# A 64-row remainder product for each of two weights, placed in the two halves of the TensorE array

## The chip, the cores and the metric

The kernel runs on one core of a Trainium2 chip. A core has TensorE (matrix products, called PE in the profile, with its weight loads shown apart as PEld), VectorE (DVE), ScalarE (ACT), GpSimd (POOL) and SyncE (SP, which issues transfers here). The metric is the device time of one execution in microseconds (us); less is better.

## The reference

A gated linear attention (an mLSTM) runs over 768 steps for 4 batches and 8 heads of width 40. Its output, 3072 rows of 320 features, goes through a bilinear layer.

```python
# per step t, for each batch and head (m is a running maximum for stability)
C = f_stab * C + i_stab * outer(v_t, k_t)
n = f_stab * n + i_stab * k_t
y_t = sigmoid(o_gate_t) * (C @ q_t) / maximum(abs(n @ q_t), 1.0)
...
x = y.transpose(0, 2, 1, 3).reshape(3072, 320)
out = ((x @ w_a) * (x @ w_b)) @ w_out        # w_a, w_b: 320 x 1536; w_out: 1536 x 320
```

The weights come as 64-bit floats.

## The kernel before

**Attention.** The 768 steps are cut into 6 chunks of 128 steps, which with 4 batches makes 24 pieces. Each piece goes through small stages: the scores (`stage_b`, or `begin_b` for the first six pieces, whose products contract over 40 rows in the upper or the lower half of the array), the product with v (`stage_c`, or `begin_c`), the part from the carried state (`stage_i`, or `begin_i`), the update of the state (`stage_u`, whose products have 64 columns), the gating (`stage_f`), and `stage_d`, which transposes the 320 features of 128 rows to features by rows.

**The layer.** `moe_block(kb)` handles one block of two or three pieces, so 256 or 384 rows of x; there are 9 blocks, three of them with 256 rows. The 1536 columns of the weights are cut into 12 slices of 128, numbered `ff`. For each slice `up(ff)` makes two sums in PSUM (`pu`): `acc[0]` for `w_a` and `acc[1]` for `w_b`. ScalarE (for two slices VectorE) copies `acc[0]` to `g`, VectorE multiplies `acc[1]` by it, and splits the product into `gh` and `gl`. Two slices later `down` multiplies those with `w_out` into the output's sums (`pd`).

**Two words per number.** TensorE takes rounded 32-bit words (float32r in the code, f32 in the profile). So x is held as `xh`, its rounded part, and `xl`, the remainder; a weight as a high and a low part. For each full tile of 128 features three products are made: high with `xh`, high with `xl`, low with `xh`. The product of low with `xl` is left out.

**The last 64 features.** 320 features are two tiles of 128 and 64 more. `stage_f` writes those 64 twice, one copy behind the other, so that the third tile of `xh` and of `xl` has them in rows 0 to 63 and again in rows 64 to 127:

```python
nc.scalar.copy(y[:, DM:], y[:, 2 * P:DM])
```

The third weight tile (`rests`) has, for `w_a`, the high part in rows 0 to 63 and the low part in rows 64 to 127, and for `w_b` the other way round:

```python
for j in range(2):
    rows, other = (slice(64 * i, 64 * i + 64) for i in (j, 1 - j))
    nc.scalar.copy(w[rows, j], W[rows])
    nc.vector.tensor_tensor(w[other, j], pc[rows], W[rows], op=ALU.add)
```

One full-height product of this tile with `xh` thus gives high and low at once. A second one with `xl` gives high with `xl`, and low with `xl` besides. Each `up(ff)` has 2 x 8 = 16 products.

**Order.** `moe_block` and the attention are generators. The main loop takes one step of `moe_block` (one product) at a time and, by a running count (`acc += units / (total * 0.93)`, where `total` is 12 x (16 + 3 x pieces)), steps of the attention in between. The framework's scheduler then settles the order of each engine's instructions from what has been written and a model of time. PSUM for `pu` is a ring of three banks.

Of the kernel before, what the change touches and what calls it, by code (L numbers as in the profile page):

```python
# [20 lines left out]
def kernel(  # L21
# [82 lines left out]
    x = ident[0:BH, 0:BH].rearrange("k (x j) -> k x j", j=2)  # L104
# [245 lines left out]
    def w_up(ff, kt, j):  # L350

        cols = slice(ff % 3 * P, (ff % 3 + 1) * P)
        if kt == 2:
            return ws[STAGES * (ff // 3) + 4][:, j, cols]
        w = ws[STAGES * (ff // 3) + 2 * kt + j]
        return w[:, 0, cols], w[:, 1, cols]

    def w_down(ff):
        w = ws[STAGES * (ff // 3) + 5 + ff % 3]
        return w[:, 0], w[:, 1]  # L360
# [3 lines left out]
    def need(x):  # L364

        while ready[0] < x:
            next(conv)
# [398 lines left out]
    def moe_block(kb):  # L766
        NT = sizes[kb] * P
        xh, xl = (x[..., 0:NT] for x in xt.pop(kb))
        pd = [ps_dn.tile([P, 512], F32, tag=f"pd{t}", name=f"pd{kb}_{t}") for t in range(sizes[kb])]
        gs = {}  # L770

        def down(ff):
            need(STAGES * (ff // 3) + 6 + ff % 3)
            gh, gl = gs.pop(ff)
            for t in range(sizes[kb]):
                cols = slice(t * P, (t + 1) * P)
                wh, wl = w_down(ff)
                for a, w, first, last in (
                    (gh, wh, True, False), (gh, wl, False, False), (gl, wh, False, True)
                ):  # L780
                    nc.tensor.matmul(  # L781
                        pd[t][:, 0:DM], a[:, cols], w,
                        start=(ff == 0 and first), stop=(ff == NF - 1 and last),
                    )
                    yield
            if ff == NF - 1:
                for t in range(sizes[kb]):
                    c, b = chunks[begins[kb] + t]
                    o = mpool.tile([P, NTB], F32, tag="acp", name=f"o{kb}_{t}")[:, 0:DM]
                    nc.scalar.copy(o, pd[t][:, 0:DM])  # L790
                    nc.sync.dma_start(out[b * S + c * P:b * S + (c + 1) * P, :], o)

        def up(ff):
            need(STAGES * (ff // 3) + 5)
            busy = hot[0] > 0
            hot[0] -= 1
            acc = [
                ps_up.tile([P, NTB], F32, tag="pu", name=f"pu{kb}_{ff}_{j}")[:, 0:NT]
                for j in range(2)
            ]  # L800
            for j in range(2):
                terms = []
                for kt in range(2):
                    h, l = w_up(ff, kt, j)
                    terms += [(h, xh[:, kt, :]), (h, xl[:, kt, :]), (l, xh[:, kt, :])]

                h = w_up(ff, 2, j)
                terms += [(h, xh[:, 2, :]), (h, xl[:, 2, :])]
                for x, (a, r) in enumerate(terms):
                    nc.tensor.matmul(  # L810
                        acc[j], a, r, start=(x == 0), stop=(x == len(terms) - 1),
                    )
                    yield
                if j == 0:
                    g = mpool.tile([P, NTB], F32, tag="acp", name=f"g{kb}_{ff}")[:, 0:NT]
                    (nc.vector.tensor_copy if ff in [1, 2] else nc.scalar.copy)(g, acc[0])  # L816
            nc.vector.tensor_tensor(g, acc[1], g, op=ALU.mult)  # L817
            gh = mpool.tile([P, NTB], F32R, tag="gh", name=f"gh{kb}_{ff}")[:, 0:NT]
            nc.vector.tensor_copy(gh, g)  # L819
            gl = mpool.tile([P, NTB], F32R, tag="gl", name=f"gl{kb}_{ff}")[:, 0:NT]  # L820
            (nc.gpsimd if kb * 12 + ff < 16 else nc.vector).tensor_tensor(  # L821
                gl, g, gh.bitcast(F32), op=ALU.subtract
            )
            gs[ff] = (gh, gl)

        LAG = 2
        for ff in range(NF + LAG):
            if ff < NF:
                yield from up(ff)
            if ff >= LAG:  # L830
                yield from down(ff - LAG)
# [286 lines left out]
```

## Time and profile before

| | |
|---|---|
| median of three runs | 565.53 us (559.82 to 567.49) |
| the profiled execution's own time | 560.51 us |
| its span, first to last instruction | 558.5 us |
| TensorE clock granted, mean | 0.993 |
| PE busy | 544.9 us (98%), 4925 instructions |
| weight loads busy (PEld) | 518.0 us (93%) |
| VectorE busy | 389.4 us (70%) |
| ScalarE busy | 267.9 us (48%) |
| GpSimd busy | 126.9 us (23%) |

The profile shows one execution. Products overlap in the array, so a busy time of PE counts the overlap once, and a product's listed duration (0.33 us for 384 columns, say) is longer than the step from its start to the next one's start. It is the step that a stream of products costs. A plain float32 product (not the rounded kind) stands as two records. The difference between the execution's own time and the span, 2.0 us, lies around the first and the last instruction.

### The profile page before, as it was taken

The numbers are of one execution on the slowest core, as the hardware profiler recorded it, in microseconds if no ns is written. First come the engines' busy times: TensorE is split into PE (matmuls) and PEld (weight loads), VectorE is DVE, ScalarE is ACT, GpSimd is POOL, SyncE is SP. The second block draws the span as 40 slices with busy tenths as digits, with TensorE's granted clock in tenths as the row PEclk, the third lists the DMA queues.
The fourth block names the chain that finished last, engine by engine and source line by source line (L and its number), as shares of the span: only waits on it lengthen the run. The fifth ranks groups of instructions, "written<-read, shape, count | busy, mean of one in ns | idle before, by whom it ended". The sixth has DMA issues, their size and how long they took to land.

```text
span 558.5 us, 12726 instructions
## 1 busy us (share of the span) xinstructions
PE 544.9 (98%) x4925; PEld 518.0 (93%) x4925; DVE 389.4 (70%) x888; ACT 267.9 (48%) x645; POOL 126.9 (23%) x188
## 2 busy tenths in 40 slices
PE   8999999899999999999999999999999999999997
PEld 6898898799999899999989999998999999999997
DVE  6889999964858683968749774977757755944332
ACT  5574678752626761556525654644526733310111
POOL 3102414641232320332031330333021302000000
PEclk9799999999999999999999999999999999999999
DMA  9999941393649762569536684586539704200001
GB/s 191 215 263 291 290 72 51 94 179 71 108 103 193 141 139 58 123 142 180 107 99 156 108 151 115 118 145 138 118 97 154 144 0 115 48 1 25 0 1 35
DMA packets 198551, 66.75 MB, mean 120 GB/s; under 512 B 184220, under 2 KB 191772, under 8 KB 198492
## 3 DMA queue, kind: packets, MB, share of 16 engines
q1 hardware_dynamic: 198444, 65.86, 56.4%
q8 instruction: 38, 0.62, 0.5%
q14 instruction: 21, 0.17, 0.1%
q10 hardware_dynamic: 48, 0.10, 0.0%
HBM read 41.11 MB, written 5.95 MB: 84 GB/s over the span
## 4 chain that ended last, share of the span: by engine, by line
PE 60%; DMA 17%; DVE 10%; ACT 5%; issue 3%; SPq 3%; POOL 1%; ACTq 0%; DVEq 0%; POOLq 0%
PE pu L810 31%; PE pd L781 15%; DMA T<-qks 4%; DMA c_dram<-cb 3%; ACT gbc L490 3%; DMA va<-in_v_dram 2%; PE pV L603 2%; PE pU L628 2%; DVE gbc L554 2%; DMA gbc<-g_dram 1%; DMA raw<-in_moe_w_a_dram 1%; DVE pb L556 1%; PE pS L884 1%; PE pV L927 1%; PE pS L545 1%
## 5 line engine op out<-in xcount | busy, mean ns | idle before, releaser
L810 PE MATMUL pu<-xh,w 128*128 128x384 f32 (+1 forms) x1080 | 276.5, 324 | 2.6 <-ACT g L816 0.9
L810 PE MATMUL pu<-xl,w 128*128 128x384 f32 (+1 forms) x648 | 208.0, 322 | 0.0
L810 PEld LDWEIGHTS pu<-xh,w 128*128 128x128 f32 x1080 | 190.6, 189 | 5.9 <-ACT g L816 1.3
L781 PE MATMUL pd<-w,gh 128*128 128x320 f32 x576 | 126.7, 309 | 0.0
L810 PEld LDWEIGHTS pu<-xl,w 128*128 128x128 f32 x648 | 122.2, 189 | 0.2
L817 DVE TENSOR_TENSOR g<-pu,g 128x384 f32<-128x384 f32 (+1 forms) x108 | 54.6, 505 | 89.4 <-PE pu L810 46.3
L781 PEld LDWEIGHTS pd<-w,gh 128*128 128x128 f32 x576 | 96.7, 188 | 0.1
L781 PE MATMUL pd<-w,gl 128*128 128x320 f32 x288 | 85.3, 310 | 0.0
L816 ACT COPY g<-pu 128x384 f32<-128x384 f32 (+1 forms) x90 | 39.6, 440 | 93.4 <-PE pu L810 84.2
L490 ACT ACTIVATE gbc<-gbc,gtab 128x128 f32<-128x128 f32 x160 | 49.1, 389 | 18.1 <-POOL gbc L483 18.0
L821 DVE TENSOR_TENSOR gl<-g,gh 128x384 fp32r<-128x384 f32 (+1 forms) x92 | 52.2, 568 | 1.9
L781 PEld LDWEIGHTS pd<-w,gl 128*128 128x128 f32 x288 | 53.1, 188 | 0.2
L585 POOL TENSOR_TENSOR vw<-va,gtab 128x336 f32<-128x336 f32 x20 | 16.4, 822 | 160.3 <-PE pU L628 135.2
L819 DVE CAST gh<-g 128x384 fp32r<-128x384 f32 (+1 forms) x108 | 41.1, 382 | 2.2
L483 POOL TENSOR_SCALAR_AFFINE_SELECT gbc<-gbc 128x1024 f32<-128x1024 f32 x20 | 22.6, 1132 | 65.1 <-DMA gbc<-g_dram 32.9
L554 DVE TENSOR_TENSOR gbc<-gbc,pb 128x512 f32<-128x512 f32 x36 | 27.2, 757 | 6.8 <-ACT pb L552 6.6
L603 PEld LDWEIGHTS <-pb 128*128 128x128 bf16 x576 | 23.4, 96 | 6.4 <-DVE pb L556 3.2
L684 POOL TENSOR_TENSOR osig<-osig,den 128x320 f32<-128x320 f32 x22 | 16.6, 754 | 54.9 <-DVE den L671 42.9
L603 PE MATMUL pV<-va,pb 128*128 128x42 bf16 x288 | 25.9, 183 | 2.7 <-DVE pb L556 2.7
L790 ACT COPY o<-pd 128x320 f32<-128x320 f32 x24 | 8.8, 434 | 40.3 <-PE pd L781 40.3
L550 DVE TENSOR_TENSOR gbc<-pS,gbc 128x512 f32<-128x512 f32 x36 | 23.7, 682 | 4.0 <-PE pS L545 4.0
L518 ACT COPY qks<-qks 128x640 bf16<-128x640 bf16 x36 | 26.0, 725 | 0.6
(154 smaller groups left out, 849.6 us busy)
## 6 DMA issues: line engine op xcount, KB each, us to landing
gbc<-g_dram SPq DMA_DIRECT2D x20, 512.0 KB
q<-in_q_dram SPq DMA_DIRECT2D x24, 160.0 KB
k<-in_k_dram SPq DMA_DIRECT2D x24, 160.0 KB
va<-in_v_dram SPq DMA_DIRECT2D x24, 160.0 KB
osig<-in_o_gate_dram SPq DMA_DIRECT2D x24, 160.0 KB
raw<-in_moe_w_out_dram SPq DMA_DIRECT2D x12, 320.0 KB
out_dram<-o SPq DMA_DIRECT2D x24, 160.0 KB
raw<-in_moe_w_a_dram SPq DMA_DIRECT2D x8, 384.0 KB
```

The lines of the kernel that those rows point to most:

```text
L483: nc.gpsimd.affine_select(E, E, pattern=[[0, H], [1, P]], compare_op=ALU.is_ge, fill=-1e30, base=0, channel_multiplier=-1,)
L490: nc.scalar.activation(E[:, h], E[:, h], AF.Exp, bias=beta[:, h:h + 1])
L518: nc.scalar.copy(qks[:, 0, :, lo:lo + 2 * D], qks[:, 1, :, D - lo:3 * D - lo])
L550: nc.vector.tensor_tensor(E, pS, E, op=ALU.mult)
L554: nc.vector.tensor_tensor(E, E, pb[:, 0], op=ALU.subtract)
L603: nc.tensor.matmul(pv[:, h], pb[i][:, h % HH, :], vb[j][:, h], start=(x == 0), stop=(x == len(terms) - 1),)
L781: nc.tensor.matmul(pd[t][:, 0:DM], a[:, cols], w, start=(ff == 0 and first), stop=(ff == NF - 1 and last),)
L810: nc.tensor.matmul(acc[j], a, r, start=(x == 0), stop=(x == len(terms) - 1),)
L816: (nc.vector.tensor_copy if ff in [1, 2] else nc.scalar.copy)(g, acc[0])
L817: nc.vector.tensor_tensor(g, acc[1], g, op=ALU.mult)
L819: nc.vector.tensor_copy(gh, g)
L821: (nc.gpsimd if kb * 12 + ff < 16 else nc.vector).tensor_tensor(gl, g, gh.bitcast(F32), op=ALU.subtract)
```

## The change

For the third tile, the product of the weights with `xl` no longer uses all 128 rows. For `w_a` it takes rows 0 to 63 of the weights and of `xl`, for `w_b` rows 64 to 127: the high part alone in each case. The program gives these products half-height tiles of 64 x 128 at array row 0 and at row 64. The one for `w_a` stays the last of its sum; the one for `w_b` is now the first of its own sum, and no step of the generator lies between the two, so they are written one behind the other. The number of products stays 16 for each slice; the generator's steps for a slice fall from 16 to 15 (`total` is not changed).

```diff
                 h = w_up(ff, 2, j)
-                terms += [(h, xh[:, 2, :]), (h, xl[:, 2, :])]
+                rows = slice(64 * j, 64 * j + 64)
+                half_k = [(h[rows], xl[rows, 2, :])]
+                terms = terms + [(h, xh[:, 2, :])]
+                terms = terms + half_k if j == 0 else half_k + terms
                 for x, (a, r) in enumerate(terms):
                     nc.tensor.matmul(
                         acc[j], a, r, start=(x == 0), stop=(x == len(terms) - 1),
                     )
-                    yield
+                    if j == 1 or x < len(terms) - 1:
+                        yield
```

**TensorE in the last block, slice 5** (names are sum slice and weight, `pu_5_0` for `w_a` and `pu_5_1` for `w_b`, then the moving operand and the weight tile). Before:

```order
L810 MATMUL pu_5_0_7782<-xl_7092,w_849 128x384
L810 MATMUL pu_5_0_7782<-xh_7091,w_849 128x384
L810 MATMUL pu_5_0_7782<-xh_7091,w_869 128x384
L810 MATMUL pu_5_0_7782<-xl_7092,w_869 128x384
L810 MATMUL pu_5_1_7783<-xh_7091,w_839 128x384
L810 MATMUL pu_5_1_7783<-xl_7092,w_839 128x384
L810 MATMUL pu_5_1_7783<-xh_7091,w_839 128x384
```

Here the fourth row is the full-height product of the third tile with `xl` for `w_a`; that for `w_b` ends its own sum, four rows further on. In the changed program the same place reads:

```order
L813 MATMUL pu_5_0_7782<-xl_7097,w_845 128x384
L813 MATMUL pu_5_0_7782<-xh_7096,w_845 128x384
L813 MATMUL pu_5_0_7782<-xh_7096,w_865 128x384
L813 MATMUL pu_5_0_7782<-xl_7097,w_865 128x384
L813 MATMUL pu_5_1_7783<-xl_7097,w_865 128x384
L813 MATMUL pu_5_1_7783<-xh_7096,w_835 128x384
L813 MATMUL pu_5_1_7783<-xl_7097,w_835 128x384
```

The fourth and the fifth row are now the two half-height products, side by side, with full-height products ahead and behind. In 68 of the 108 slices they stand like this: 51 with 384 columns and 17 with 256.

**TensorE in a middle block, slice 4** (`pd` is the output's sum, `pb` and `pV` are the attention's). Before:

```order
L810 MATMUL pu_4_0_3703<-xh_2541,w_869 128x384
L810 MATMUL pu_4_0_3703<-xl_2542,w_869 128x384
L810 MATMUL pu_4_1_3704<-xh_2541,w_839 128x384
L810 MATMUL pu_4_1_3704<-xl_2542,w_839 128x384
L810 MATMUL pu_4_1_3704<-xh_2541,w_839 128x384
```

After the change:

```order
L813 MATMUL pu_4_0_3689<-xh_2544,w_865 128x384
L813 MATMUL pu_4_0_3689<-xl_2545,w_865 128x384
L781 MATMUL pd_0_3257<-w_815,gh_2_3508 128x320
L813 MATMUL pu_4_1_3690<-xl_2545,w_865 128x384
L813 MATMUL pu_4_1_3690<-xh_2544,w_835 128x384
L813 MATMUL pu_4_1_3690<-xl_2545,w_835 128x384
```

The scheduler has moved another block product, full height, between the two half-height ones. In 40 of the 108 slices something of that kind stands between them (one product in 14 slices, up to 98 rows of attention in one): 21 with 384 columns and 19 with 256.

## The prediction

> **What bounds the kernel.** I read the page first, then the chain that ended last, then what PE waited for, then rows of PE in order of time.
>
> ```profile
> span 558.5 us, 12726 instructions
> ...
> PE 544.9 (98%) x4925; PEld 518.0 (93%) x4925; DVE 389.4 (70%) x888; ACT 267.9 (48%) x645; POOL 126.9 (23%) x188
> ```
>
> PE is busy for 98% of the span and no other engine for more than 70%. Since products overlap, that alone does not say that PE streams at its best pace, so the chain of the last block is needed (start, length, what):
>
> ```profile
> 543.73 2.80 PE pu L810 x16
> 546.53 1.31 PE pd L781 x9
> 547.84 2.80 PE pu L810 x16
> ```
>
> One slice of a 384-column block is 16 + 9 products and takes 547.84 - 543.73 = 4.11 us, with nothing else on the chain. One of the 16 costs 2.80 / 16 = 0.175 us. Time put into or taken out of PE there moves the end one for one. How much slack is left elsewhere is in the list of waits (total us, times, longest):
>
> ```profile
> PE pV L603 <- DVE pb L556: 2.7, 5, 0.9
> ...
> PE pX L707 <- DVE gbc L550: 1.0, 2, 0.7
> PE pu L810 <- ACT g L816: 0.9, 1, 0.9
> PE pu L810 <- DVE g L817: 0.7, 2, 0.4
> ```
>
> These four are 5.3 us in 10 waits, all that PE waits for in the layer and the main attention but for parts of a microsecond. So the kernel is bound by PE nearly throughout, and the question is what the half-height products cost on PE.
>
> **Two half-height products side by side.** The early attention already runs them: L884 contracts over 40 rows, in the upper or lower half (start, length, what):
>
> ```profile
> 7.53 0.38 PE L884 MATMUL pS<-T 40*128 40x128 f32 x2 [0.39 <-ACT T L873]
> ...
> 7.53 1.16 PE L884 MATMUL pS<-T 40*128 40x128 f32 x16 [0.39 <-ACT T L873]
> ...
> 60.47 1.16 PE L884 MATMUL pS<-T,T 40*128 40x128 f32 x8
> ...
> 480.62 0.28 PE L810 MATMUL pu<-xh,w 128*128 128x256 f32 x1
> 480.74 1.07 PE L545 MATMUL pS<-T,T 120*128 120x128 bf16 x16
> ```
>
> At 7.53 products alternate between the halves, and 16 records take 1.16 us. At 60.47 all are in one half, and 8 records take the same 1.16 us. The first two records at 7.53 fit in 0.38 us although one lasts 0.373 (the longest duration in the next fence), so the second starts some 0.007 us after the first. At full height the 16 records of 128 columns at 480.74 start (1.07 - 0.22) / 15 = 0.057 us apart, 0.22 being the length of one. So a pair in the two halves does overlap, and its second product is nearly free: I take 0.006 us. The bound on the other side, since no rounded 32-bit product runs like this before, is one after the other, 0.174 us at 384 columns and 0.12 at 256.
>
> The Trainium skill, TensorE: Matmul & The Clock Gate, section The mechanism of its part on packing, has tiles in different rows start about 4 ns apart, which this row bears out; by it the second product would cost 0.004 us.
>
> **Going to half height and back.** Now the price of entering and leaving. First 256 columns, then 384; in the second place the other tile has 64 columns instead of 64 rows, the nearest row that follows a 384-column product:
>
> ```profile
> 86.15 0.28 PE L810 MATMUL pu<-xl,w 128*128 128x256 f32 x1
> 86.27 0.40 PE L810 MATMUL pu<-xh,w 128*128 128x256 f32 x2
> 86.51 0.28 PE L810 MATMUL pu<-xl,w 128*128 128x256 f32 x1
> 86.72 0.49 PE L884 MATMUL pS<-T,T 40*128 40x128 f32 x2
> 87.13 0.41 PE L781 MATMUL pd<-w,gh 128*128 128x320 f32 x1
> ...
> 158.90 0.34 PE L810 MATMUL pu<-xh,w 128*128 128x384 f32 x1
> 159.07 0.34 PE L810 MATMUL pu<-xl,w 128*128 128x384 f32 x1
> 159.34 0.92 PE L628 MATMUL pU<-vw,k 128*64 128x42 f32 x16
> 160.19 0.62 PE L810 MATMUL pu<-xh,w 128*128 128x384 f32 x2
> ...
> 158.90 0.19 PEld L810 LDWEIGHTS pu<-xl,w 128*128 128x128 f32 x1
> 159.34 0.80 PEld L628 LDWEIGHTS pU<-vw,k 128*64 128x64 f32 x16 [0.25 <-issue]
> 160.19 0.30 PEld L810 LDWEIGHTS pu<-xh,w 128*128 128x128 f32 x2
> ...
> L884 PE MATMUL pS<-T,T x64: 272/272/373, 32.8 to 89.2; 40*128 40x128 f32 x64
> ```
>
> (The last row is that line's shortest, median and longest duration in ns.) A visit to the other tile shape has four prices:
>
> - Entry, emptying the array. Full-height products of 256 columns start 0.12 us apart (86.15 to 86.51 is three steps); the half-height one starts 0.21 after the last: **+0.09**. With 384 columns 0.17 becomes 0.27: **+0.10**. In both the next start is the product's own length less 0.07.
> - Entry, the load. In the stream the weights of the next product are loaded under the running one: the PEld row at 158.90 is for the product at 159.07. The load at 159.34 begins only with its product. The first L884 after an entry lasts 373 ns instead of 272: **+0.10**.
> - Leaving, emptying. The two records at 86.72 cost 0.11 each (60.47: (1.16 - 0.27 - 0.10) / 7) and the first one's load 0.10; the next product starts after 0.41: **+0.09**. By the rule of the entry a 384-column product would pay +0.10.
> - Leaving, the load. At 160.19 the two products last 0.62 together; less 0.34 the second starts after 0.28 instead of 0.17: **+0.11**.
>
> Together 0.39 to 0.41 us a visit. I take 0.385 at 256 and 0.40 at 384 columns. The type of the numbers is not the cause: at 480.62 a 32-bit product is followed by a bf16 one after 0.12 us, the plain step.
>
> The Trainium skill, TensorEngine Tiling (Array Packing), section Key Properties, says the same against this change: "Changing tiling mode (not just tile) drains the TensorE". The rows above agree. The page prices neither the drain nor the load behind it; with a drain alone (0.18 to 0.20 us) the sum would be that of the second rival.
>
> **The sum.** The order of the changed program has the two half-height products adjacent in 68 slices and apart in 40.
>
> - Visits: 68 for the adjacent pairs, 2 x 40 for the others, less 3 that lie against a half-height product of the attention: 145. Of them 93 have 384 columns (51 + 42), 52 have 256 (17 + 38 - 3). 93 x 0.40 + 52 x 0.385 = **+57.2 us**.
> - Saved: only adjacent pairs overlap. 51 x (0.174 - 0.006) + 17 x (0.12 - 0.006) = **-10.5 us**. Apart, a half-height product streams as many columns as a full one and saves nothing.
> - The product of the low weights with `xl` that disappears had no instruction of its own: nothing.
> - The generator makes 12 x 24 = 288 steps in a 384-column block instead of 300, so the attention is dealt out 4% later. PE's own work beside it hides that: the attention's waits in the list are 3.7 us. Uncovered, it would be a few more of those, 0.5 to 0.9 us each.
> - Waits: no new one in steady state. `w_b`'s sum needs its bank one product earlier; in a ring of three it was freed by a copy a whole slice (4.11 us) before. ScalarE's copy and VectorE's product come later with PE and have idle time. Of the 5.3 us of waits above some go, since PE comes later to what it waited for: between 0 and -5.3, I take **-3 us**.
>
> 57.2 - 10.5 - 3 = +43.7. From the profiled execution's 560.5 us that is 604.2. The median of the three runs was 5.0 above that execution and the lowest 0.7 below; I add half of the five, less rounding: **606 us**, 7% slower than 565.5.
>
> **Rivals.**
>
> - *Not side by side after all*: the rounded products run one after the other although in two halves; then the change does not do what it says. The saved 10.5 us are gone: about 617. Against it stand the starts at 7.53; for it, that two 128-column streams in sequence (2 x 0.057) would also fit the 0.11 us at which pairs go on there.
> - *The load hides*: the half-height weights and those behind them are loaded while the array empties. Each visit costs 0.18 to 0.20 instead of 0.39: 93 x 0.20 + 52 x 0.18 = 28 less 10.5, so +17.5, and with the same 2.5 for the median 579 (-1 for waits). The PEld rows at 159.34 and 160.19 speak against it.
> - *The other side, no emptying*: between two rounded 32-bit products with the same weight tile the array goes over to half height in the running stream, as it does from bf16 to 32 bits. Then only the saving is left: 560.5 - 10.5 = 550, with 2.5 for the median 552.5, 2.3% faster. It decides below 10.5 / 145 = 0.07 us a visit. Every entry and exit quoted speaks against it, but none has rounded products on both sides.
> - *The waits take more*: all 5.3 us and part of the start go. About 602; inside the forecast.
>
> The Trainium skill, same page, section Theoretical Speedup, gives "Up to 2×" for a contraction of at most 64 rows; taken alone that is the third rival. The trace agrees only while the shape stays, as at 7.53.
>
> **How the numbers follow.** Forecast 0.74, with 597 to 614 from visits of 0.37 to 0.42 us and waits of 0 to -5.3. Not side by side 0.09, load hidden 0.09, no emptying 0.04, and 0.04 for new waits beyond 622. The range 588 to 622 takes in the first two and leaves out 0.17. Two per cent, 11 us, is about what a measurement of this kernel tells from no change. Faster by more than that: the third rival, 0.03 of its 0.04. Within: its rest and part of the second, 0.05. Slower 0.92.
>
> **What would show it.** Rows of L813 with 64*128, two of them 0.35 us long together with 384 columns and more by the load's 0.1; a start 0.27 us behind the product ahead; a first full product of about 0.44 us after each. In the last block 4.11 us per slice should become 4.11 + 0.40 - 0.17 = 4.34 where the two are adjacent, 4.11 + 0.80 = 4.91 where not. PE's busy share stays near 98%, since emptying counts as busy; PEld's falls. The prediction is wrong if half-height loads start under the product ahead, if a pair's two starts lie 0.17 apart, or if the attention falls behind and PE's waits grow beyond some 10 us.

## The result and the profile after

| | before | after |
|---|---|---|
| median of four runs | 563.87 us | 598.25 us (594.87 to 605.76) |
| the profiled execution | 560.51 us | 600.5 us |
| span | 558.5 us | 598.7 us |

The change makes the kernel **slower: ratio 1.059, 95% interval 1.047 to 1.071**. The forecast was 606 us, 588 to 622. One of the four executions after, at 605.76, was a slow one that the ratio leaves out.

The first lines of the page, and what became of the half-height products in the view of groups that keeps shapes apart:

```profile
span 598.7 us, 12729 instructions
...
PE 587.5 (98%) x4925; PEld 513.8 (86%) x4925; DVE 392.5 (66%) x888; ACT 269.2 (45%) x645; POOL 126.3 (21%) x188
...
PEclk9999979999999999999999999999999999999999
...
L813 PE MATMUL pu<-xl,w 64*128 64x384 f32 x144 | 41.0, 439 | 0.0
```

PE has as many instructions as before and is again busy for 98% of a span that is 40 us longer. Its weight loads are busy for less (86% against 93%): time has gone in which nothing is loaded. A half-height product of 384 columns lasts 0.439 us on average, a full one in the stream 0.34. PEclk is the granted clock of TensorE in tenths of full speed, in forty slices of the span.

The chain of the last block, where PE has nothing else to do (start, length, what):

```profile
583.52 3.03 PE pu L813 x15
586.55 1.31 PE pd L781 x9
587.86 3.03 PE pu L813 x15
```

A slice now takes 587.86 - 583.52 = 4.34 us, and it took 4.11. The 16 products of `up` stand here as 15, since two start together, but need 3.03 us where 16 needed 2.80. Where the 0.23 us lie is seen in the rows of PE and of the weight loads, in order of time, in the same block:

```profile
584.25 0.51 PE L813 MATMUL pu<-xh,w 128*128 128x384 f32 x2
584.70 0.44 PE L813 MATMUL pu<-xl,w 64*128 64x384 f32 x2
585.07 0.44 PE L813 MATMUL pu<-xh,w 128*128 128x384 f32 x1
585.35 0.34 PE L813 MATMUL pu<-xl,w 128*128 128x384 f32 x1
...
584.08 0.37 PEld L813 LDWEIGHTS pu<-xh,w 128*128 128x128 f32 x2
584.69 0.19 PEld L813 LDWEIGHTS pu<-xl,w 64*128 64x128 f32 x2 [0.25 <-issue]
585.07 0.19 PEld L813 LDWEIGHTS pu<-xh,w 128*128 128x128 f32 x1 [0.18 <-issue]
585.17 0.19 PEld L813 LDWEIGHTS pu<-xl,w 128*128 128x128 f32 x1
```

Two half-height products of 0.44 us fit into 0.44 us: their starts are less than 0.01 us apart, and so are their two loads. That part works. But the product ahead started at 584.25 + 0.51 - 0.34 = 584.42 or so, and the pair 0.27 behind it; the next full product starts 0.37 behind the pair, and the one after it 0.28 later. A plain step is 0.174. The idle times of the weight loads, 0.25 and 0.18 us with no release named, are the two stretches in which I take the array to empty: no weights come in and no product starts. The first product on either side then lasts 0.44 instead of 0.34; its load starts with it and not under the product ahead.

What PE waited for (total us, times, longest):

```profile
PE pd L781 <- POOL gl L825: 2.3, 1, 2.3
...
PE pu L813 <- ACT g L820: 0.8, 1, 0.8
...
PE pX L707 <- ACT cst L633: 0.3, 1, 0.3
```

Of the four waits that the list before had with 5.3 us in all, those for `pb` and `gbc` are gone, and those for `g` are down to one of 0.8 us. The 2.3 us on GpSimd's `gl` are new and lie in the first block, at 68 us. Behind this wait the granted clock is at half for 10.24 us, from 72.3 on: there products of 256 columns start 0.21 us apart, not 0.12. Before, the clock is at half for 6.8 us too, but at 18.6 us, ahead of the layer's first product.

### The profile page after: what moved, and what is told of

Same layout as the page of the kernel before. It is cut to its first block, busy times and chain, and to the rows that moved or that the text cites. A ratio compares the mean times of both kernels' runs of the same rounds, so it can differ in the third digit from the quotient of the medians.

```text
span 598.7 us, 12729 instructions
## 1 busy us (share of the span) xinstructions
PE 587.5 (98%) x4925; PEld 513.8 (86%) x4925; DVE 392.5 (66%) x888; ACT 269.2 (45%) x645; POOL 126.3 (21%) x188
## 4 chain that ended last, share of the span: by engine, by line
PE 91%; issue 3%; DVE 3%; ACT 1%; POOL 1%; DMA 1%; ACTq 0%; POOLq 0%; DVEq 0%
PE pu L813 51%; PE pd L781 22%; PE pV L603 4%; PE pS L545 3%; PE pU L628 2%; PE pX L707 1%; PE pS L888 1%; PE pI L571 1%; PE pV L931 1%; PE pc L449 1%; PE pI L908 1%; PE pT L874 1%; DMA g_i<-in_i_gate_dram 1%; PE pc L450 1%; DVE cr L426 0%
## 5 line engine op out<-in xcount | busy, mean ns | idle before, releaser
L813 PE MATMUL pu<-xh,w 128*128 128x384 f32 (+1 forms) x1080 | 285.5, 334 | 0.0
L813 PE MATMUL pu<-xl,w 128*128 128x384 f32 (+3 forms) x648 | 202.0, 355 | 0.8 <-ACT g L820 0.8
L813 PEld LDWEIGHTS pu<-xl,w 128*128 128x128 f32 (+1 forms) x648 | 109.8, 188 | 29.0 <-issue 20.7
L781 PE MATMUL pd<-w,gh 128*128 128x320 f32 x576 | 132.0, 317 | 0.5 <-DVE gh L823 0.5
L823 DVE CAST gh<-g 128x384 fp32r<-128x384 f32 (+1 forms) x108 | 39.0, 361 | 2.0
L483 POOL TENSOR_SCALAR_AFFINE_SELECT gbc<-gbc 128x1024 f32<-128x1024 f32 x20 | 24.1, 1203 | 49.4 <-DMA gbc<-g_dram 48.1
L603 PEld LDWEIGHTS <-pb 128*128 128x128 bf16 x576 | 23.5, 96 | 4.3 <-issue 3.1
L686 ACT COPY osig<-osig 128x64 f32<-128x64 f32 x22 | 5.4, 244 | 48.3 <-DVE osig L685 48.1
```

Of the source, the lines that this page charges most:

```text
L483: nc.gpsimd.affine_select(E, E, pattern=[[0, H], [1, P]], compare_op=ALU.is_ge, fill=-1e30, base=0, channel_multiplier=-1,)
L603: nc.tensor.matmul(pv[:, h], pb[i][:, h % HH, :], vb[j][:, h], start=(x == 0), stop=(x == len(terms) - 1),)
L781: nc.tensor.matmul(pd[t][:, 0:DM], a[:, cols], w, start=(ff == 0 and first), stop=(ff == NF - 1 and last),)
L813: nc.tensor.matmul(acc[j], a, r, start=(x == 0), stop=(x == len(terms) - 1),)
```

## The experiments

Three theories were set against each other. **A**: every visit to the half height costs about 0.39 us, and a pair side by side gives 0.17 back. **B**: the moved order (40 slices with work between the two, another dealing of the attention) made the loss. **C** says that the two halves do not overlap.

**The change with full-height products again.** One line of the changed kernel:

```diff
-                half_k = [(h[rows], xl[rows, 2, :])]
+                half_k = [(h, xl[:, 2, :])]
```

> The changed kernel with both remainder products at full height again: they stay the last product of w_a's sum and the first of w_b's, and the generator makes the 15 steps a slice of the change. TensorE's order agrees with that of the change in 99 of 100 products, and no product of the layer is half-height. Theory A (0.39 us for each visit): the time of before, 558 to 566 us, so that the whole loss of the change lies in the visits. Theory B (the moved order has a part in it, as it had when both products were put at the slice's end): between 570 and 598.

Measured: 563.3 us against 561.2 for the kernel before, ratio 1.004 (1.000 to 1.008). So the order and the 15 steps account for some 2 us of the 34, for 5 at most by the interval, and theory B falls as the cause of the loss. Between this kernel and the change only the height of two products in 16 differs, and in one product of 100 the order that the scheduler chose. What the order does cost lies in the first block: in the profiled execution the second block begins 4.7 us later than before (114.86 against 110.13 us), and from there to the end the two differ by 0.2 us. The wait for `gl` is here too, and behind it the clock at half, from 68.8 us on, again for 10.24 us:

```profile
PE pd L781 <- POOL gl L825: 2.7, 1, 2.7
...
PEclk9999969999999999999999999999999999999999
```

**Half height in the order of before.** Here the program's order of products is that of before throughout, and each remainder product stays last in its own sum, so no pair forms.

```diff
-                terms += [(h, xh[:, 2, :]), (h, xl[:, 2, :])]
+                rows = slice(64 * j, 64 * j + 64)
+                terms += [(h, xh[:, 2, :]), (h[rows], xl[rows, 2, :])]
```

> The order of before, each remainder product last in its own sum, but half-height: 216 visits less a few, no pair. Theory A: 72 x 2 x 0.40 + 36 x 2 x 0.385 = 85 paid, less up to 8 of waits: 637 to 650 us. Theory B: the time of before, 560 to 570. Were the price the emptying alone (0.18 to 0.20): 600 to 607.

Measured: 632.2 us, ratio 1.130 (1.124 to 1.137), 72 us slower. Then the same with `w_a`'s product alone (`rows` is all 128 for `j == 1`):

> The order of before to the instruction, and only w_a's remainder product half-height: 108 visits, no pair. Theory A: half of what 216 visits cost in this order, 72 x 0.40 + 36 x 0.385 = 42.7 less up to 6 of waits: 596 to 604 us. If the first visit of a slice did the damage and the second came cheap (a rival to a price per visit): 610 or more. If waits hid the first visits: below 590.

Measured: 592.9 us, ratio 1.057 (1.051 to 1.062), 32 us slower: 108 visits cost 32, 216 cost 72. Both miss the expected range by 3 to 5 us on the cheap side. The chains of the last block, first with two visits to a slice, then with one:

```profile
614.08 3.38 PE pu L811 x16
617.45 1.51 PE pd L781 x9
618.96 3.38 PE pu L811 x16
```

```profile
570.82 3.20 PE pu L811 x16
574.02 1.31 PE pd L781 x9
575.34 3.20 PE pu L811 x16
```

4.88 us and 4.52 us a slice, beside 4.11 with none: 0.77 for two visits and 0.41 for one in these rows, 0.39 a visit over the whole block. So where PE alone sets the time the price per visit is as forecast, and the shortfall lies elsewhere. Measured from the first product of each block to that of the next, the last block grows by 9.4 us with 24 visits and by 4.75 with 12, which is 0.39 to 0.40 each; blocks 2 to 5 (numbered from 0) grow by 7.4 to 8.0 and by 2.8 to 3.5. There 1.2 to 2.1 us in a block are hidden, whether 12 or 24 visits are paid. Those are blocks with attention, and before, PE waited in them.

**Both at the slice's end, full height.** The next three kernels put the two remainder products last in the slice and issue them together, so that nothing can come between:

```diff
+            with tc.issue_after(last), tc.high_priority(4000):
+                for j in range(2):
+                    product(j, 7, *ends[j])
```

> Both remainder products stand at the end of the slice, side by side, as full-height products: no visit to the half height, 83 stretches of equal tile shape in the program's order against 81 before. Theory A (the price is 0.39 us for each visit to the half height, the gain 0.168 us for each overlapped pair of 384 columns and 0.114 of 256): no change from before, 560 to 567 us. Theory B (the loss comes from the moved order and the changed dealing of the attention): still clearly slower than before, above 575.

Measured: 583.5 us, ratio 1.039 (1.031 to 1.047). A miss for theory A, and the number lies where B had it. But this is not the change's order, which at full height cost little; it is an order with a loss of its own. `acc[0]` ends 7 products later, so its copy to `g` comes late, and PE waits for it:

```profile
PE pu L802 <- ACT g L822: 7.3, 7, 1.9
PE pc L449 <- ACT g L822: 2.4, 1, 2.4
...
PEclk9799989799999999999999998999999899999999
```

The granted clock, 0.978 over the span against 0.993 before, dips in five of the forty slices of the span, where it dipped in one before: it is at half there for 3.4 or 6.8 us at a time. So the next two are to be compared with this kernel and with each other, and the last block tells more than the whole.

**All 108 pairs together.**

> The same order as with full-height products at the slice's end, but in the two halves; all 108 pairs stand together: 108 visits. Theory A: 72 x 0.40 + 36 x 0.385 = 42.7 paid, 72 x 0.168 + 36 x 0.114 = 16.2 saved, so 26 above the full-height version less up to 6 of waits that go: 583 to 592 us, faster than the change by 8 to 14. Theory B: as the full-height version in this order. Theory C (the two halves do not overlap): 600 to 606.

Measured: 598.7 us, ratio 1.069 (1.064 to 1.074). Outside the expected 583 to 592, for the base itself stands 20 us higher than I took it. Above that base it is 15 us, where 20 to 26 were expected; where the rest went was not traced. The last block:

```profile
580.79 3.03 PE pu L802 x15
583.82 1.31 PE pd L781 x9
585.13 3.03 PE pu L802 x15
```

4.34 us again, as in the change. Keeping all pairs together does not make the change pay.

**Both in one half.** As the last, but `w_b`'s product also takes rows 0 to 63.

> As the version with all pairs together, but both products use rows 0 to 63, so w_b's sum gets its low weights times xl in place of the high ones. 108 visits, no overlap. Theory A: 16 us slower than the pairs in two halves, 599 to 608. Theory C: the same time as the pairs.

Measured: 608.1 us, ratio 1.086 (1.081 to 1.091), 9.4 us slower than the pairs in two halves. PE in order of time and the chain:

```profile
586.74 0.62 PE L802 MATMUL pu<-xl,w 64*128 64x384 f32 x2
587.29 0.44 PE L802 MATMUL pu<-xh,w 128*128 128x384 f32 x1
```

```profile
581.03 3.23 PE pu L802 x16
584.26 1.31 PE pd L781 x9
585.57 3.23 PE pu L802 x16
```

The two now take 0.62 us where the pair took 0.44: the second starts 0.28 behind the first, not at once. A slice takes 4.54 us against 4.34, so the overlap is worth 0.20 us, and theory C falls. Over the whole kernel only 9.4 of the expected 16 us show. Part of it is waits: those for `g` are 8.8 us with the pairs and 5.8 in one half. The granted clock of the two profiles differs too (0.981 and 0.992): with the pairs it is at half for 20.5 us in all ahead of the end, in one half for 10.2. How the rest divides was not settled.

**Can a visit be saved elsewhere?** The kernel before pays such visits too: the update of the state (L628) has tiles of 64 columns. Two heads' keys as 128 stationary columns avoid them, at the price of products of which half is thrown away:

```diff
-        for h in (*range(0, H, 2), *range(1, H, 2)):
-            nc.tensor.matmul(pu[r:r + 64, x], nat(n)[0][1][:, h, :], vw[:, h], ...)
+        for x in range(HH):
+            nc.tensor.matmul(pu[:, x], nat(n)[0][1][:, 2 * x:2 * x + 2, :], vw[:, 2 * x:2 * x + 2], ...)
```

> The kernel before, with the state's update (L628) rid of its 64-column tiles: each product takes the keys of two heads as 128 stationary columns and both heads' values as 84 moving ones, and the two useful quarters of the result are read out. 80 products of full shape in place of 160 of 64 columns; the program changes the array's shape 35 times instead of 80. Theory A, with a price for every change of shape: the update of a piece takes 1.06 us of TensorE's stream before (from 0.17 behind the product at 159.07 to 0.11 behind that at 160.19) and 8 records at 0.112 = 0.90 after, so 0.16 x 20 = 3 us less, up to 6 with the early pieces whose updates stand in several parts: 555 to 559 beside 561. If 64-column tiles are entered and left for nothing: 0.90 against 16 records in 0.69, 4 us slower.

Measured: 573.1 us, ratio 1.021 (1.017 to 1.025). The same kernel once more, for its profile:

> The same kernel as the last, for a profile at TensorE's usual pace: the one taken has steps between products nearly twice as long throughout. If the 64-column tiles are entered for nothing, L628 takes 0.90 us a piece in place of 0.69 and the loss of 13 us lies there only in small part (4 us). If the changes of shape have their price, L628 gains and the loss lies in waits or in the order around it.

Measured: 572.9 us, ratio 1.023 (1.017 to 1.029). A miss again: slower, not faster. One update does take less of PE, 0.89 us instead of 1.06 where it follows a 384-column product; where it follows the attention's own `pV`, as most do, it gains only 0.07. But the scheduler made the order of the first two blocks anew, and block 2 begins 12.2 us later than before (163.84 against 151.68 us), with waits such as these:

```profile
PE pS L889 <- DVE osig L690: 4.4, 1, 4.4
...
PE pS L545 <- DMA T<-qks: 3.5, 1, 3.5
```

The granted clock is at half there for 10.24 us from 68.9 and for 3.4 us from 126.9. From block 2 on this kernel takes 0.8 us more than before. The last run keeps the old form for the first eight pieces, and with it the old order:

> Full-shape products for the state's update from piece 8 on only; TensorE's order is that of before up to there, so the early pieces cannot move. 12 pieces times 0.17 us (1.06 less the 0.89 measured for one piece in the last run): 2.0 us less than before, 557 to 560 beside 560, if the waits in the middle blocks stay as they are; up to 3 more or less if they don't.

Measured: 563.6 us beside 558.2, ratio 1.006 (1.003 to 1.009). A miss, if a small one. In the profiled execution blocks 1 and 2 begin within 0.1 us of where they began before; afterwards nothing is gained (span 559.0 against 558.5). The 12 updates save 1.1 us and not 2.0: 4 of them gain some 0.15 us, 8 stand behind `pV` and gain 0.07. The waits from block 2 on are 5.1 us where they were 4.9, so they have hardly grown, but the longest is 1.4 us where it was 0.9:

```profile
PE pV L603 <- DVE pb L556: 2.9, 2, 1.4
PE pu L825 <- ACT g L831: 1.6, 2, 0.8
...
PEclk9999999999999999999999899999999999999999
```

Behind the wait of 1.4 us the granted clock is at half from 317.9 us on, for 3.41 us, and products of 384 columns start 0.32 us apart instead of 0.17. That block, number 4, grows by 1.1 us, which is as much as all the updates save.

None of the versions beats the kernel before.

## Why the prediction was right, point by point

- **PE bounds.** Right. With 216 visits PE has no wait over 0.3 us left in blocks 2 to 6, and the time is PE's stream alone.
- **Entry and exit.** Right, the two middle terms (load on entry, emptying on exit) as a sum. For 384 columns the trace after has 0.268 from the product ahead to the half-height one (+0.094), 0.368 from there to the next (+0.194: emptying and load) and 0.278 from that to the one behind it (+0.104): 0.39 us a visit (0.395 from the product ahead to the second one behind), where 0.40 was taken. For 256 columns 0.209, 0.310 and 0.223: 0.38, where 0.385 was taken. That 40-row products of another number type and 64-column tiles were the nearest rows did no harm. The Trainium skill's sentence on draining at a change of tiling mode (TensorEngine Tiling (Array Packing), Key Properties) holds here also between products of one type. The loads behind the two drains are half of the price.
- **Side by side.** Right: starts 0.003 us apart in the median, against 0.006 taken, and 0.20 us a slice lost when it is undone.
- **The count.** Slightly off: 66 pairs stand together in the trace, not 68, and 84 products alone. In two slices of the first block (from 58.5 and from 107.3 us) seven full-height products of the slice stand between the two. Less four that lie against half-height work of the attention there are 146 visits: 93 x 0.395 + 53 x 0.382 = 57.0 us, less 51 x 0.171 + 15 x 0.117 = 10.5, so +46.5 where the sum had +46.7. (Eleven of these visits end at a `pV` product and cost some 0.09 less, 1.0 us in all.)
- **The waits: the term that was mis-sized.** I took -3 us, at most -5.3, from the list of waits. The list counts a wait only from the modelled end of the product ahead, some 0.16 us behind the point at which the next could have started. From start to start the steps over 0.3 us too long in blocks 2 to 6 add up to 6.3 us before, and all of them are gone after. The whole of it shows from the first product of block 1 to the end, where the granted clock is full in each of these executions. There the change pays 40.9 us net by the prices above, and 31.6 show against before; with 216 visits 75.2 are paid and 65.2 show, with 108 it is 37.6 and 29.2. So 8 to 10 us are hidden each time: a stock of slack and not a share of the price. Where the part of it beyond the 6.3 us lay was not traced.
- **The order: put at nothing.** Block 1 begins 8.6 us later than before, and the products ahead of it pay 5.6 of that. The other 3.0 I put down to the order: the wait of 2.3 us for `gl` and the stretch at half clock behind it, which the full-height kernel of this order has too. The sum had no term for it, while its term for the waits was some 6 us too small: 46.5 - 9.3 + 3.0 = 40.2 us, which is what the two spans differ by, where the sum had 43.7. That the two partly cancel was luck.
- **The median.** I added half of the gap of 5 us between the profiled execution and the median. The profiled execution after, at 600.5, stands above its median, so this went the wrong way. The narrower range's low end of 597 is slightly off as well: 145 visits of 0.37 us less 10.5 and 5.3 give 598.4, before anything is added for the median.
- **The rivals.** No emptying and a hidden load are both refuted by the rows at 584.69 and 585.07: the pair starts 0.27 behind the product ahead, and the loads begin with their products. One product after the other is refuted by the run in one half. That the waits take more, 602, came nearer to the measured 598 than the forecast of 606.
- **What would show it** came as named: 4.34 us a slice in the last block, rows of 0.44 us, a start 0.27 behind the product ahead, loads busy for less. In the sentence there, 4.91 us for two visits is 4.88 to 4.90.

## What to carry to other kernels

Two half-height products side by side save one product's step (0.17 us here), but entering and leaving the shape costs 0.39 us at 384 columns and 0.38 at 256. By these prices, an estimate that no run tried, at least three pairs of 384 columns would have to share a visit before it pays; each slice here has one pair. Read the price from any place where the kernel already changes shape: both starts around it, and the first product's length. And where another chain makes an engine wait, added work is partly hidden and saved work need not be gained; what PE's waits are worth is read from start to start, together with the granted clock behind them.

## What the runs showed of the hardware that I had not expected

The price of a visit hardly depends on the columns: 0.38 us at 256 and 0.39 at 384. When a short bf16 product follows the visit, the second load is nearly free: the step behind it is 0.039 us instead of 0.025 (L603), against 0.278 instead of 0.174 for a 384-column product.

The granted clock fell to half behind some of PE's waits: for 10.24 us behind waits of 2.3 us (the change) and 2.7 us (its order at full height), for 3.41 us behind one of 1.4 us (the last run). There the steps were 0.21 us instead of 0.12 at 256 columns and 0.32 instead of 0.17 at 384, so such a wait cost more in the products behind it than in itself. What sets it off is not shown. A wait of 1.6 us at 265 us in the run with both products at the slice's end was followed by no drop, and in the profiled execution with 216 visits the clock was at half from 92.5 to 113.0 us with no wait listed near it.
